# Sliding-window attention into a gated feed-forward: the third half's q and k transposed by TensorE instead of the DMA crossbar, and the fourth half's loads placed behind wo

## The chip, the cores and the metric

The kernel runs on one core of one Trainium2 chip. The metric is the device time of one execution in microseconds (us), and less is better. The kernel before takes 266.46 us (median of three runs, 266.06 to 266.63). The profile comes from one further execution, which has a time of its own.

## The reference, cut to what matters

Four batches, eight heads, 768 positions and a head size of 64. Every query sees eight global keys and the 96 most recent ones, with a linear bias by distance. The result is laid out as 3072 tokens of 512 numbers and goes through a feed-forward of width 1536 with a gate.

```
keep   = is_global | ((rel >= 0) & (rel < 96))        # rel = query position - key position
scores = q @ k.T / sqrt(64) - slope_of_head * dist
a      = softmax(where(keep, scores, -1e9))
x      = (a @ v) laid out as [3072, 512]
out    = (relu(x @ w_gate) * (x @ w_val)) @ w_out
```

All inputs and the output are float32; the kernel computes in bf16 with float32 accumulation.

## The kernel before, in words

**Halves and chunks.** The queries are cut into eight halves `s` = 0..7 of 384 positions, two for each batch. A half's attention gives `xT[s]`, 512 by 384, and this is the input of feed-forward chunk `c = s`. A chunk has 24 first-layer items (a `gate` and a `val` for each of twelve groups of 128 columns, four matmuls of 384 columns each, L479 and L489) and six `outp` items (six matmuls of 512 columns each, L498), of which two make one block of 128 output rows. The result of an `outp` pair is copied to `osb` (two buffers) and stored by SP. The first-layer weights come in three groups of four (`wg[0..2]`, `wv[0..2]`), the second-layer weight `wo_sb` in one DMA of its own, all issued by POOL, which also casts them to bf16 on the way.

**How q and k get into shape.** The matmul that makes the scores needs q and k with the head dimension on the partitions, and they arrive with positions there. There are two ways in the kernel.
- Halves 0 and 1: `piece_cast` casts a pair of heads to bf16, `piece_t` transposes it with six TensorE matmuls against the identity (L281) into an `av_ps` bank, and DVE copies q to `qT` (L285) and the keys to their places in `kT` (`put_keys`, L265 to L271).
- Halves 2 to 7: `piece_cast_k` and `piece_cast_q` cast on POOL into `kc` and `qz` (L289, L297; `qz` has zeros beside each head, so that two heads of a pair go through one matmul), three DMA transposes each on SP's queue bring them to `kN` and `qT` (`piece_xk` L300, `piece_xq` L304), and `piece_order` copies the keys from `kN` to `kT`, on DVE for half 2 and on POOL for the others.

**Attention itself.** Halves 0 and 1 add the bias with matmuls (`piece_bias`, L330) ahead of the score matmuls (`piece_score`, L347); later halves multiply by a mask after the exponential (`piece_qk`, L365 to L377). `piece_av` (L393) and `piece_av_wide` (L427) multiply by v; the sums go through ACT as Ln and Exp of its negative, and DVE multiplies the result into `xT` (L410, L438).

**What sets the order.** The schedule is written out by hand: the order of the calls is the order on each engine, and SP, POOL, DVE, ACT and PE each work through their own list. `weave` runs a list of feed-forward items and puts other pieces between them, each at a share of the list's estimated time. After half 0's attention there are these stages:
- **first weave**: group 0 of chunk 0 and the first two items of group 1 (ten items), with the attention of half 1;
- **second weave**: group 0 of chunk 1, the rest of group 1 of chunk 0, and group 1 of chunk 1 (22 items); in the kernel before it holds nothing else for PE;
- **third weave**: group 2 of both chunks (16 items), then the `outp` items of both (12 items), with the attention of half 2;
- **then** one weave for each of the chunks 2 to 7, with the attention of the next half and the casts and transposes of the one after.

Between the first and the second weave stand the preparations for halves 2 and 3, which mostly concern POOL and SP: weight group 2, q and k of halves 2 and 3 (`load_qk_after`: a tiny memset of the buffer on POOL, behind which the loads on SP wait), the zeros, the casts and transposes of both halves, v, and the load of `wo_sb`.

Of the kernel before, what the change touches and what calls it, by code (L numbers as in the profile page):

```python
# [15 lines left out]
def kernel(  # L16
# [12 lines left out]
    nc = tc.nc  # L29

    B, H, S, D = q.shape
# [8 lines left out]
    NN = 3  # L40
# [200 lines left out]
    def piece_cast(s, p):  # L241
        qk = cast_pool.tile([128, 2, NN, 2, D], BF16, name="qk")
        cast_of[s, p] = qk
        for i, src in ((1, ks_of[s]), (0, qs_of[s])):
            copy = nc.gpsimd.tensor_copy
            if s == 0:
                copy = (nc.vector.tensor_copy, nc.scalar.copy, nc.scalar.copy, nc.vector.tensor_copy)[p]
            elif p > 0:
                copy = (nc.vector.tensor_copy, nc.scalar.copy)[p % 2]
            copy(  # L250
                qk[:, i].rearrange("t n e d -> t e n d"),
                src[:, 2 * p : 2 * p + 2, :].rearrange("t e (n d) -> t e n d", n=NN))

    def put_keys(copy, copy_small, kt, src, half):

        tk = src.rearrange("d (n p) -> d p n", n=NN)

        def put(j0, j1, p0, r0, r1):
            o = kt[:, j0:j1, r0:r1].rearrange("d j (p n) -> d j p n", n=NN)
            np_ = (r1 - r0) // NN  # L260
            i_ = tk[:, p0 : p0 + (j1 - j0) * np_, :].rearrange("d (j p) n -> d j p n", j=j1 - j0)
            return o, i_

        if half == 0:
            copy(*put(0, 3, 0, NG, 128))  # L265
            copy_small(*put(3, 4, 120, NG, NG + 24))
            copy_small(kt[:, :, 0:NG], kt[:, 0:1, NG : 2 * NG].to_broadcast([128, NT, NG]))
        else:
            copy(*put(4, 6, 32, NG, 128))
            copy_small(*put(3, 4, 0, NG + 24, 128))  # L270
            copy_small(*put(6, 7, 112, NG, NG + 48))  # L271

    def piece_t(s, p):
        b, half = divmod(s, 2)
        kt = kT[b % 2][p]
        qk = cast_of[s, p]
        tp = av_psum.tile([128, 512], FP32, name="av_ps")
        tp = tp[:, 0:QH].bitcast(BF16).rearrange("d (i t) -> d i t", i=2)
        for i in range(2):
            for n in range(NN):  # L280
                nc.tensor.matmul(tp[:, i, n * 128 : (n + 1) * 128],  # L281
                                 lhsT=qk[:, i, n],
                                 rhs=ident, is_transpose=True,
                                 start=(i == 0 and n == 0), stop=(i == 1 and n == NN - 1))
        nc.vector.tensor_copy(qTb[s][:, p, 0, :], tp[:, 0, :])  # L285
        put_keys(nc.vector.tensor_copy, nc.vector.tensor_copy, kt, tp[:, 1, :], half)

    def piece_cast_k(s, p):
# [18 lines left out]

    def piece_order(s, p):
        b, half = divmod(s, 2)
        copy = nc.vector.tensor_copy if s == 2 else nc.gpsimd.tensor_copy  # L310
        put_keys(copy, copy, kT[b % 2][p], kNb[s % 2][:, p], half)

    def early_pieces(s):
        out = [(0.0, lambda p=p: piece_cast_k(s, p)) for p in range(HP)]
# [122 lines left out]
            xT_of[s] = xt_pool.tile([128, N_DC, QH], BF16, name="xT")  # L437
        nc.vector.tensor_tensor(xT_of[s][:, p, :], av[1][:, 0:QH], rc, op=ALU.mult)  # L438

    def attention_pieces(s):  # L440
        T = lambda p: [(0.34, lambda: piece_t(s, p))]
        QK = lambda p: [(0.18, lambda g=g: piece_qk(s, p, g)) for g in range(3)]
        AW = lambda p: [(0.58, lambda: piece_av_wide(s, p))]
        C = lambda p: [(0.0, lambda: piece_cast(s, p))]
        BI = lambda p, *gs: [(0.2, lambda g=g: piece_bias(s, p, g)) for g in gs]
        SC = lambda p, *gs: [(0.2, lambda g=g: piece_score(s, p, g)) for g in gs]
        X = lambda *fs: [(0.0, f) for f in fs]
        if s == 0:
            return (C(0) + X(lambda: load_v_globals(0), lambda: load_v(0, 0), lambda: load_v(0, 1),
                             lambda: load_v(0, 2), lambda: load_v(0, 3), lambda: load_w_group(0))  # L450
                    + C(1) + T(0) + BI(0, 0, 1) + C(2) + T(1) + SC(0, 0, 1) + BI(1, 0) + SC(1, 0) + C(3) + T(2)
                    + BI(1, 1) + SC(1, 1) + BI(2, 0) + T(3) + X(lambda: copy_v_globals(0, 1, 4))
                    + SC(2, 0) + BI(2, 1) + SC(2, 1)
                    + BI(3, 0) + SC(3, 0) + BI(3, 1) + SC(3, 1)
                    + AW(0) + AW(1) + X(lambda: load_qk_after(1, nc.vector, True)) + AW(2)
                    + AW(3) + X(second_pools, lambda: warm(4)))
        if s == 1:
            return (C(1) + C(2) + T(0) + BI(0, 0, 1) + T(1) + C(3) + SC(0, 0, 1) + T(2) + BI(1, 0) + SC(1, 0) + BI(1, 1)
                    + SC(1, 1) + T(3) + BI(2, 0) + SC(2, 0) + BI(2, 1) + AW(0) + SC(2, 1) + BI(3, 0)
                    + SC(3, 0) + AW(1) + BI(3, 1) + SC(3, 1) + AW(2) + AW(3))  # L460
        AV = lambda p: [(0.29, lambda e=e: piece_av(s, p, e)) for e in range(2)]
        g = QK(3)
        a = AV(2)
        return (QK(0) + QK(1) + AV(0) + QK(2) + AV(1) + g[0:1] + a[0:1] + g[1:2] + a[1:2] + g[2:3]
                + [(0.0, lambda: None)] * 2 + AV(3))
# [51 lines left out]
    def spread(items, first, last):  # L517

        n = len(items)
        return [(first + (i + 0.5) / n * (last - first), f) for i, (_, f) in enumerate(items)]  # L520
# [25 lines left out]
    f1_0, f2_0 = ffn_pieces(0)  # L546
    f1_1, f2_1 = ffn_pieces(1)
    G = [slice(2 * GW * i, 2 * GW * (i + 1)) for i in range(N_FC // GW)]
    g0 = f1_0[G[0]]
    weave(g0[0::2] + g0[1::2] + f1_0[G[1]][0:2], spread(attention_pieces(1), 0.4, 0.98))  # L550
    other_pools()
    load_w_group(2)
    load_qk_after(2, nc.gpsimd)
    load_qk_after(3, nc.gpsimd)
    for p in range(HP):
        nc.gpsimd.memset(kT[1][p][:, 3, 32:128].bitcast(mybir.dt.uint32), 0)
        nc.gpsimd.memset(kT[1][p][:, 6, NG + 48 : 128].bitcast(mybir.dt.uint32), 0)
    nc.gpsimd.memset(vbuf[1][:, NT - 1, :].bitcast(mybir.dt.uint32), 0)
    for i in range(2):
        nc.gpsimd.memset(qz[i].rearrange("t n p e z -> t (n p e z)").bitcast(mybir.dt.uint32), 0)  # L560
    for j in range(NT):
        fill_ones(nc.gpsimd, 1, j)
    load_v_globals(1)
    for _, f in early_pieces(2)[:-HP]:
        f()
    spread_v_globals(1)
    load_v_half(2)
    e3 = early_pieces(3)[:-HP]
    for _, f in e3[:HP]:
        f()  # L570
    load_w(wo_sb, moe_w_out, 0, DM)
    for _, f in e3[HP:]:
        f()
    load_v_half(3)
    weave(f1_1[G[0]] + f1_0[G[1]][2:] + f1_1[G[1]],
          [(0.1 + 0.1 * h, lambda h=h: mask(h)) for h in range(H)])
    weave(f1_0[G[2]] + f1_1[G[2]] + f2_0 + f2_1,
          [(0.02 + 0.05 * p, lambda p=p: piece_order(2, p)) for p in range(HP)],
          spread(attention_pieces(2), 0.25, 0.9), [(0.95, lambda p=p: piece_order(3, p)) for p in range(HP)],
          [(0.55 + 0.05 * j, lambda j=j: fill_ones(nc.vector, 0, j)) for j in range(NT)])  # L580

    for c in range(2, NHALF):
# [44 lines left out]
```

## Time and profile before

| what | value |
|---|---|
| time, median of three runs | 266.46 us (266.06 to 266.63) |
| the profiled execution: its own time | 264.71 us |
| its span, first to last instruction | 262.7 us |
| PE busy (TensorE matmuls) | 243.4 us, 93% of the span |
| ACT busy | 159.6 us, 61% |
| DVE busy | 127.5 us, 49% |
| POOL busy | 85.7 us, 33% |
| mean granted TensorE clock | 0.985 of full |
| moved by DMA | 34.31 MB, 131 GB/s over the span |

The profiled execution lasted 2.0 us longer than its span, and 1.75 us less than the median of the timed runs. A row of the timeline gives the start, the time from the first start to the last end of a group of like instructions, the engine, the line, the operation with its tiles, the count, and in brackets the idle time just before and what ended it. Matmuls overlap in the pipe, so the cost of one group of matmuls is read from its start to the start of the next. A row of the windows gives, for a stretch of time, the busy time of PE, PE's weight loads, DVE, ACT and POOL with the number of instructions, then the granted clock, the mean busy share of the DMA engines (it can exceed 1 where packets overlap) and the GB/s.

### The profile page before, as it was taken

How to read it: one execution, taken by the hardware profiler on the slowest of the kernel's cores; microseconds unless marked ns; L12 is line 12 of the kernel's file. 1: busy time of each engine (PE TensorE's matmuls, PEld its weight loads, DVE VectorE, ACT ScalarE, POOL GpSimd, SP SyncE). 2: the span in 40 equal slices, each digit the busy share in tenths (PEclk: the TensorE clock that was granted, in tenths of full speed). 3: DMA queues.
4: the chain of work that ended last, by engine and by line, in shares of the span. 5: the costliest groups of instructions: out<-in, count | busy, mean ns of one | idle time of the engine just before them, and what ended most of it. 6: DMA issues, size and time to landing. Idle time of an engine off the chain costs nothing.

```text
span 262.7 us, 4849 instructions
## 1 busy us (share of the span) xinstructions
PE 243.4 (93%) x1727; PEld 142.7 (54%) x1727; DVE 127.5 (49%) x328; ACT 159.6 (61%) x321; POOL 85.7 (33%) x213
## 2 busy tenths in 40 slices
PE   7888769995699999999999999999999999999993
PEld 3655555662345556655655566655665566556641
DVE  3646424472406556752667166625573356714410
ACT  5876575732438568755776477756875678653311
POOL 7808903990021516430164505800550000000000
PEclk9999999998979999999999999999999999999999
DMA  6999999999992496773744995864771200021012
GB/s 192 140 220 213 180 232 311 184 140 156 152 169 95 94 230 183 154 59 114 229 109 88 120 295 90 132 75 120 223 159 44 80 0 2 1 80 42 0 40 80
DMA packets 82264, 34.31 MB, mean 131 GB/s; under 512 B 58177, under 2 KB 79169, under 8 KB 82241
## 3 DMA queue, kind: packets, MB, share of 16 engines
q1 hardware_dynamic: 50384, 26.11, 40.8%
q0 software_dynamic: 31856, 7.91, 32.4%
q8 instruction: 13, 0.21, 0.4%
q14 instruction: 11, 0.08, 0.1%
HBM read 28.38 MB, written 6.29 MB: 132 GB/s over the span
## 4 chain that ended last, share of the span: by engine, by line
PE 66%; DMA 17%; ACT 6%; DVE 5%; POOL 2%; issue 2%; SPq 1%; ACTq 0%; DVEq 0%
PE ff_ps L498 24%; PE ff_ps L489 16%; PE ff_ps L479 15%; DMA qs<-in_q_dram 8%; DMA wo_sb<-in_moe_w_out_dram 7%; PE av_ps L393 5%; PE qk_ps L365 4%; DVE xT L410 2%; DMA ks<-in_k_dram 2%; SPq L131 1%; ACT es L352 1%; ACT rcp L407 1%; ACT lnd L402 1%; DVE ht L491 1%; POOL vbuf L155 1%
## 5 line engine op out<-in xcount | busy, mean ns | idle before, releaser
L489 PE MATMUL ff_ps<-xT,wv 128*128 128x384 bf16 x384 | 78.7, 328 | 2.1 <-DMA wv<-in_moe_w_val_dram 1.2
L479 PE MATMUL ff_ps<-xT,wg 128*128 128x384 bf16 x384 | 78.5, 327 | 1.5 <-DMA wg<-in_moe_w_gate_dram 1.2
L498 PE MATMUL ff_ps<-wo_sb,ht 128*128 128x512 bf16 x288 | 68.4, 384 | 2.9 <-DMA wo_sb<-in_moe_w_out_dram 2.9
L482 ACT ACTIVATE grelu<-ff_ps 128x384 bf16<-128x384 f32 x96 | 47.1, 490 | 35.2 <-PE ff_ps L479 18.0
L491 DVE TENSOR_TENSOR ht<-ff_ps,grelu 128x384 bf16<-128x384 f32 x96 | 53.2, 555 | 29.9 <-PE ff_ps L489 24.1
L479 PEld LDWEIGHTS <-wg 128*128 128x128 bf16 x384 | 36.5, 98 | 25.7 <-DMA wg<-in_moe_w_gate_dram 1.9
L489 PEld LDWEIGHTS <-wv 128*128 128x128 bf16 x384 | 36.3, 98 | 25.2 <-issue 3.1
L410 DVE TENSOR_TENSOR xT<-av_ps,rcp 64x384 bf16<-64x384 f32 x48 | 26.6, 555 | 46.4 <-ACT rcp L407 45.7
L368 ACT ACTIVATE es<-qk_ps 128x432 bf16<-128x432 f32 (+2 forms) x72 | 37.9, 528 | 18.3 <-PE qk_ps L365 16.4
L377 DVE TENSOR_TENSOR es<-es,m_all 128x432 bf16<-128x432 bf16 (+5 forms) x108 | 31.1, 316 | 30.8 <-ACT es L368 30.3
L498 PEld LDWEIGHTS <-ht 128*128 128x128 bf16 x288 | 27.1, 98 | 31.8 <-DMA wo_sb<-in_moe_w_out_dram 3.3
L503 ACT COPY osb<-ff_ps 128x512 f32<-128x512 f32 x24 | 14.1, 586 | 26.2 <-PE ff_ps L498 25.3
L402 ACT ACTIVATE lnd<-av_ps 64x384 f32<-64x384 f32 x48 | 23.3, 485 | 10.4 <-PE av_ps L393 9.6
L289 POOL CAST kc<-ks 128x384 bf16<-128x384 f32 x24 | 11.4, 521 | 54.7 <-DMA ks<-in_k_dram 47.6
L365 PE MATMUL qk_ps<-qT,kT 128*128 128x432 bf16 (+5 forms) x108 | 25.4, 292 | 2.6 <-DMA qT<-qz 2.6
L155 POOL DMA_DIRECT2D vbuf<-in_v_dram x28 | 24.4, 880 | 0.4 <-issue 0.3
L393 PEld LDWEIGHTS <-vbuf 128*128 128x128 bf16 x216 | 18.3, 99 | 8.1 <-issue 0.8
L393 PE MATMUL av_ps<-es,vbuf 128*128 128x216 bf16 (+4 forms) x216 | 21.5, 227 | 0.2 <-DVE xT L410 0.2
L365 PEld LDWEIGHTS <-kT 128*128 128x128 bf16 x108 | 10.7, 99 | 11.1 <-DMA qT<-qz 3.0
L297 POOL CAST qz<-qs 128x192 bf16<-128x192 f32 x48 | 14.6, 356 | 5.2 <-DMA qs<-in_q_dram 4.7
L407 ACT ACTIVATE rcp<-lnd 128x384 f32<-128x384 f32 x24 | 12.5, 523 | 0.8
L352 ACT ACTIVATE es<-qk_ps 128x864 bf16<-128x864 f32 (+3 forms) x16 | 10.6, 708 | 3.5 <-PE qk_ps L347 3.5
(77 smaller groups left out, 131.7 us busy)
## 6 DMA issues: line engine op xcount, KB each, us to landing
out_dram<-osb SPq DMA_DIRECT2D x24, 256.0 KB
ks<-in_k_dram SPq DMA_DIRECT2D x6, 768.0 KB
qs<-in_q_dram SPq DMA_DIRECT2D x6, 768.0 KB
vbuf<-in_v_dram POOLq DMA_DIRECT2D x24, 120.0 KB, 4.6
ks<-in_k_dram SPq DMA_DIRECT2D x8, 192.0 KB
qs<-in_q_dram SPq DMA_DIRECT2D x8, 192.0 KB
wg<-in_moe_w_gate_dram POOLq DMA_DIRECT2D x3, 512.0 KB, 7.8
wv<-in_moe_w_val_dram POOLq DMA_DIRECT2D x3, 512.0 KB, 10.8
```

The lines of the kernel that those rows point to most:

```text
L155: nc.gpsimd.dma_start(out=v_dst(b, NG + r0, NG + r0 + n, j), in_=v[b, :, KT * j + r0 : KT * j + r0 + n, :].rearrange("h p d -> p h d"))
L365: nc.tensor.matmul(ps[:, c : c + n_], lhsT=kt[:, j, :], rhs=qd[:, :, :, a : a + w], start=True, stop=True)
L368: nc.scalar.activation(es[:, 0:cols], ps[:, 0:cols], AF.Exp, bias=0.0, scale=scale)
L377: nc.vector.tensor_mul(e4, e4, mk)
L393: nc.tensor.matmul(av3[:, :, a : a + w], lhsT=vb[:, j, z0 : z0 + 128], rhs=es[:, c : c + NN * w].rearrange("k (n p) -> k n p", n=NN), star ...
L402: nc.scalar.activation(ln[o0 : o0 + 64], av[d0 : d0 + 64, 0:QH], AF.Ln, bias=0.0, scale=1.0)
L410: nc.vector.tensor_tensor(xT_of[s][r, p, :], av_of[s, p, e_][r, 0:QH], rc[r], op=ALU.mult)
L479: nc.tensor.matmul(psg[:, 0:QH], lhsT=w_of(wg, dc, fc), rhs=xT[:, dc, :], start=(dc == 0), stop=(dc == N_DC - 1))
L482: nc.scalar.activation(gr, psg[:, 0:QH], AF.Relu, bias=0.0, scale=1.0)
L489: nc.tensor.matmul(psv[:, 0:QH], lhsT=w_of(wv, dc, fc), rhs=xT[:, dc, :], start=(dc == 0), stop=(dc == N_DC - 1))
L491: nc.vector.tensor_tensor(ht[:, fc, :], psv[:, 0:QH], st[fc], op=ALU.mult)
L498: nc.tensor.matmul(ps2, lhsT=ht[:, fc, n * 128 : (n + 1) * 128], rhs=wo_sb[:, fc, :], start=(fc == 0), stop=(fc == N_FC - 1))
```

## The change

- `piece_cast` runs on POOL for all four pairs of half 2, and `piece_t` also serves half 2: it writes q in two copies of 64 partitions, one for each head of the pair, into a `qT[0]` whose other halves POOL has set to zero. The four `piece_t` of half 2 stand in the second weave at 0.50, 0.64, 0.78 and 0.92 of it. Half 2 no longer uses `kc`, `qz`, `kN`, the six DMA transposes and `piece_order`.
- q and k of half 2 are loaded in four pairs of heads (eight DMAs) instead of two whole DMAs.
- q and k of half 3 are no longer loaded at the start of the second weave, but at 0.25 of the third, behind a memset on DVE. Its casts, v, transposes and `piece_order` follow in the third weave, at 0.40 to 0.45, 0.45, 0.52 to 0.56 and 0.64 to 0.68, and 0.93 to 0.97.
- On POOL the load of `wo_sb` stands behind the casts and the v of half 2, and nothing of half 3 is ahead of it.
- In the first weave the four `val` items of group 0 and the two items of group 1 take other places among the attention pieces of half 1.
- The attention of half 2 starts at 0.20 of the third weave instead of 0.25.

```diff
@@ piece_cast
             if s == 0:
                 copy = (nc.vector.tensor_copy, nc.scalar.copy, nc.scalar.copy, nc.vector.tensor_copy)[p]
-            elif p > 0:
+            elif s == 1 and p > 0:
                 copy = (nc.vector.tensor_copy, nc.scalar.copy)[p % 2]
@@ piece_t
-        nc.vector.tensor_copy(qTb[s][:, p, 0, :], tp[:, 0, :])
+        if s < 2:
+            nc.vector.tensor_copy(qTb[s][:, p, 0, :], tp[:, 0, :])
+        else:
+            for e in range(2):
+                r = slice(64 * e, 64 * e + 64)
+                nc.vector.tensor_copy(qTb[s % 2][r, p, e, :], tp[r, 0, :])
@@ piece_order
-        copy = nc.vector.tensor_copy if s == 2 else nc.gpsimd.tensor_copy
-        put_keys(copy, copy, kT[b % 2][p], kNb[s % 2][:, p], half)
+        put_keys(nc.gpsimd.tensor_copy, nc.gpsimd.tensor_copy, kT[b % 2][p], kNb[s % 2][:, p], half)
@@ attention_pieces
-    def attention_pieces(s):
+    def attention_pieces(s, vals=(), more=()):
...
         if s == 1:
-            return (C(1) + C(2) + T(0) + BI(0, 0, 1) + T(1) + C(3) + SC(0, 0, 1) + T(2) + BI(1, 0) + SC(1, 0) + BI(1, 1)
-                    + SC(1, 1) + T(3) + BI(2, 0) + SC(2, 0) + BI(2, 1) + AW(0) + SC(2, 1) + BI(3, 0)
-                    + SC(3, 0) + AW(1) + BI(3, 1) + SC(3, 1) + AW(2) + AW(3))
+            v = [[x] for x in vals]
+            m = [[x] for x in more]
+            return (C(1) + C(2) + T(0) + BI(0, 0, 1) + v[0] + C(3) + T(1) + SC(0, 0, 1) + v[1] + T(2)
+                    + BI(1, 0) + SC(1, 0) + BI(1, 1) + SC(1, 1) + v[2] + T(3) + BI(2, 0) + SC(2, 0)
+                    + BI(2, 1) + AW(0) + v[3] + SC(2, 1) + BI(3, 0) + SC(3, 0) + AW(1)
+                    + BI(3, 1) + SC(3, 1) + m[0] + AW(2) + m[1] + AW(3))
@@ the stages
-    g0 = f1_0[G[0]]
-    weave(g0[0::2] + g0[1::2] + f1_0[G[1]][0:2], spread(attention_pieces(1), 0.4, 0.98))
+    for _, f in f1_0[0:2 * GW:2]:
+        f()
+    for _, f in attention_pieces(1, f1_0[1 : 2 * GW : 2], f1_0[2 * GW : 2 * GW + 2]):
+        f()
     other_pools()
     load_w_group(2)
-    load_qk_after(2, nc.gpsimd)
-    load_qk_after(3, nc.gpsimd)
+    load_qk_after(2, nc.gpsimd, True)
...
-    for i in range(2):
-        nc.gpsimd.memset(qz[i].rearrange("t n p e z -> t (n p e z)").bitcast(mybir.dt.uint32), 0)
+    for e in range(2):
+        nc.gpsimd.memset(qTb[0][64 - 64 * e : 128 - 64 * e, :, e, :].bitcast(mybir.dt.uint32), 0)
...
     load_v_globals(1)
-    for _, f in early_pieces(2)[:-HP]:
-        f()
+    for p in range(HP):
+        piece_cast(2, p)
+    load_v_half(2)
+    load_w(wo_sb, moe_w_out, 0, DM)
     spread_v_globals(1)
-    load_v_half(2)
-    e3 = early_pieces(3)[:-HP]
-    for _, f in e3[:HP]:
-        f()
-    load_w(wo_sb, moe_w_out, 0, DM)
-    for _, f in e3[HP:]:
-        f()
-    load_v_half(3)
+    for i in range(2):
+        nc.gpsimd.memset(qz[1 - i].rearrange("t n p e z -> t (n p e z)").bitcast(mybir.dt.uint32), 0)
+    e3 = early_pieces(3)
+    ck, xk, cq, xq, od = e3[0:HP], e3[HP : HP + NN], e3[HP + NN : 2 * HP + NN], e3[2 * HP + NN : -HP], e3[-HP:]
     weave(f1_1[G[0]] + f1_0[G[1]][2:] + f1_1[G[1]],
-          [(0.1 + 0.1 * h, lambda h=h: mask(h)) for h in range(H)])
+          [(0.1 + 0.1 * h, lambda h=h: mask(h)) for h in range(H)],
+          [(0.5 + 0.14 * p, lambda p=p: piece_t(2, p)) for p in range(HP)])
     weave(f1_0[G[2]] + f1_1[G[2]] + f2_0 + f2_1,
-          [(0.02 + 0.05 * p, lambda p=p: piece_order(2, p)) for p in range(HP)],
-          spread(attention_pieces(2), 0.25, 0.9), [(0.95, lambda p=p: piece_order(3, p)) for p in range(HP)],
+          spread(attention_pieces(2), 0.2, 0.9), [(0.25, lambda: load_qk_after(3, nc.vector))],
+          spread(ck + cq, 0.4, 0.45), [(0.45, lambda: load_v_half(3))],
+          spread(xk, 0.52, 0.56), spread(xq, 0.64, 0.68), spread(od, 0.93, 0.97),
           [(0.55 + 0.05 * j, lambda j=j: fill_ones(nc.vector, 0, j)) for j in range(NT)])
```

What this does to the lists of the engines is seen at three places. The first is POOL's list behind the global rows of v (L141) up to the end of v for half 3; `kc` and `qz` are the operands of the DMA transposes, `qk` that of `piece_t`, and a row with a count stands for that many calls. In the kernel before:

```order
L289 CAST kc_112<-ks 128x2x3x64 x4
L297 CAST qz_110<-qs 128x3x64 x8
L155 DMA vbuf_96<-in_v_dram 120x8x64 x4
L289 CAST kc_113<-ks 128x2x3x64 x4
L172 DMA wo_sb<-in_moe_w_out_dram 128x12x512
L297 CAST qz_111<-qs 128x3x64 x8
L155 DMA vbuf_96<-in_v_dram 120x8x64 x2
```

In the changed kernel (the last of the four pairs of casts is shown, the three like it stand ahead):

```order
L250 CAST qk<-ks 128x2x3x64
L250 CAST qk<-qs 128x2x3x64
L155 DMA vbuf_96<-in_v_dram 120x8x64 x4
L172 DMA wo_sb<-in_moe_w_out_dram 128x12x512
L578 MEMSET qz_111 128x1536
L294 CAST kc_113<-ks 128x2x3x64 x4
L302 CAST qz_111<-qs 128x3x64 x8
L155 DMA vbuf_96<-in_v_dram 120x8x64 x2
```

The casts of half 3's k no longer stand ahead of the load of `wo_sb`; all of half 3's work is behind it.

The second place is SP's list, from the last loads of half 2 to the first stores of the output. In the kernel before, where `kc_112`, `qz_110` belong to half 2 and `kc_113`, `qz_111` to half 3:

```order
L131 DMA ks<-in_k_dram 128x8x192
L131 DMA qs<-in_q_dram 128x8x192
L300 DMA_TRANSPOSE kN_108<-kc_112 128x4x128 x3
L304 DMA_TRANSPOSE qT_106<-qz_110 128x8x128 x3
L146 DMA vbuf_96<-vbuf_96 8x8x64 x6
L300 DMA_TRANSPOSE kN_109<-kc_113 128x4x128 x3
L304 DMA_TRANSPOSE qT_107<-qz_111 128x8x128 x3
L504 DMA out_dram<-osb 128x512 x6
```

In the changed kernel:

```order
L146 DMA vbuf_96<-vbuf_96 8x8x64 x6
L131 DMA ks<-in_k_dram 128x8x192
L131 DMA qs<-in_q_dram 128x8x192
L511 DMA out_dram<-osb 128x512
L305 DMA_TRANSPOSE kN_109<-kc_113 128x4x128 x2
L511 DMA out_dram<-osb 128x512
L305 DMA_TRANSPOSE kN_109<-kc_113 128x4x128
L309 DMA_TRANSPOSE qT_107<-qz_111 128x8x128
L511 DMA out_dram<-osb 128x512
L309 DMA_TRANSPOSE qT_107<-qz_111 128x8x128 x2
L511 DMA out_dram<-osb 128x512 x3
```

The six transposes of half 2 are gone, and those of half 3, which stood ahead of all stores of the first two chunks, now stand between them, behind the loads of their own half.

The third place is DVE's list from the last `piece_t` of half 1 to the keys of the first pair of half 2; `ht` is the product of a `val` item, `xT` that of an attention pair. In the kernel before:

```order
L271 COPY kT_3_101<-av_ps 128x48
L438 TENSOR_TENSOR xT<-av_ps,rcp 128x384 x2
L491 TENSOR_TENSOR ht<-ff_ps,grelu 128x384
L438 TENSOR_TENSOR xT<-av_ps,rcp 128x384 x2
L491 TENSOR_TENSOR ht<-ff_ps,grelu 128x384 x11
L265 COPY kT_0_102<-kN_108 128x3x120
```

In the changed kernel:

```order
L271 COPY kT_3_101<-av_ps 128x48
L442 TENSOR_TENSOR xT<-av_ps,rcp 128x384
L498 TENSOR_TENSOR ht<-ff_ps,grelu 128x384
L442 TENSOR_TENSOR xT<-av_ps,rcp 128x384 x2
L498 TENSOR_TENSOR ht<-ff_ps,grelu 128x384
L442 TENSOR_TENSOR xT<-av_ps,rcp 128x384
L498 TENSOR_TENSOR ht<-ff_ps,grelu 128x384 x5
L290 COPY qT_106<-av_ps 64x384 x2
L265 COPY kT_0_102<-av_ps 128x3x120
```

There is one more `val` product among the attention pairs of half 1 than before, and the one that stood between the second and the third pair (the `val` of group 1) stands between the third and the fourth. The keys of half 2 come from the PSUM bank of `piece_t` instead of `kN`, after five of the eleven products of the second weave instead of after all of them.

## The prediction

> **What bounds the kernel now.** I read the page first, then PE's waits, then stretches of time, then PE's timeline where the waits lie. The page:
>
> ```profile
> span 262.7 us, 4849 instructions
> PE 243.4 (93%) x1727; PEld 142.7 (54%) x1727; DVE 127.5 (49%) x328; ACT 159.6 (61%) x321; POOL 85.7 (33%) x213
> ```
>
> PE is the bound, and 19.3 us of the span are left that it is not busy. PE's longest waits for DMA:
>
> ```profile
> PE ff_ps L498 <- DMA wo_sb<-in_moe_w_out_dram: 2.9, 1, 2.9
> PE qk_ps L365 <- DMA qT<-qz: 2.6, 1, 2.6
> ```
>
> Each happens once, for `wo_sb` and for the transposed q of half 2, both in the third weave. Windows of the first weave and around the two waits (PE, PEld, DVE, ACT and POOL busy, then granted clock, DMA share, GB/s):
>
> ```profile
> 16.13:39.84 23.71, 18.59 (x234) 12.28 (x231) 10.57 (x30) 14.94 (x28) 12.76 (x32) 1.00 1.19 216
> ...
> 61.45:69.70 8.25, 5.62 (x27) 2.83 (x26) 2.21 (x7) 3.27 (x7) 0.00 (x0) 0.79 1.33 168
> 69.70:77.67 7.97, 5.05 (x23) 2.45 (x23) 1.77 (x5) 1.57 (x5) 1.97 (x7) 0.79 1.60 149
> 77.67:93.66 15.99, 15.77 (x95) 8.13 (x94) 8.37 (x23) 10.92 (x22) 5.43 (x10) 1.00 0.55 117
> ```
>
> The first weave leaves PE 5.1 us idle, at a full clock. In the two rows in the middle two things cost time: the waits, and a granted clock of 0.79 over each stretch. In the last row, still the third weave, the clock is 1.00 and PE is busy for 15.77 of 15.99 us. PE's timeline there:
>
> ```profile
> 60.64 0.81 PE L479 MATMUL ff_ps<-xT,wg 128*128 128x384 bf16 x4
> 64.09 0.54 PE L365 MATMUL qk_ps<-qT,kT 128*128 128x432 bf16 x1 [2.63 <-DMA qT<-qz]
> ...
> 67.32 0.81 PE L489 MATMUL ff_ps<-xT,wv 128*128 128x384 bf16 x4
> ...
> 68.62 0.35 PE L365 MATMUL qk_ps<-qT,kT 128*128 128x432 bf16 x1
> 68.80 0.81 PE L489 MATMUL ff_ps<-xT,wv 128*128 128x384 bf16 x4
> 69.45 0.35 PE L365 MATMUL qk_ps<-qT,kT 128*128 128x432 bf16 x1
> 72.72 1.71 PE L498 MATMUL ff_ps<-wo_sb,ht 128*128 128x512 bf16 x6 [2.92 <-DMA wo_sb<-in_moe_w_out_dram]
> ...
> 77.67 1.46 PE L498 MATMUL ff_ps<-wo_sb,ht 128*128 128x512 bf16 x6
> ...
> 79.33 1.46 PE L498 MATMUL ff_ps<-wo_sb,ht 128*128 128x512 bf16 x6
> 80.63 0.31 PE L365 MATMUL qk_ps<-qT,kT 128*128 128x288 bf16 x2
> 80.78 0.42 PE L393 MATMUL av_ps<-es,vbuf 128*128 128x216 bf16 x4
> 81.05 1.46 PE L498 MATMUL ff_ps<-wo_sb,ht 128*128 128x512 bf16 x6
> ```
>
> From start to start at full clock: a gate or val item 0.65 (68.80 to 69.45), a score matmul 0.18 (68.62 to 68.80) or 0.15 for the pair of small ones (80.63 to 80.78), an `outp` item 1.30 (79.33 to 80.63), an AV piece 0.27 (80.78 to 81.05).
>
> **The two waits of the third weave, with their slow clock.** The item at 60.64 costs 0.65, so PE could go on at 61.29; it does at 64.09: 2.80 lost. Between 64.09 and 67.32 stand three scores and two items, 0.18 + 0.65 + 0.18 + 0.65 + 0.15 = 1.81; they take 3.23: 1.42 lost to the clock. At 69.45 + 0.18 = 69.63 PE could start on `outp`; it does at 72.72: 3.09. From there to 77.67 stand two `outp` items, a score pair and two AV pieces, 2.60 + 0.15 + 0.54 = 3.29; they take 4.95: 1.66. In all 2.80 + 1.42 + 3.09 + 1.66 = 8.97 us. The change aims at both waits. The first goes if q of half 2 is there in time, the second if `wo_sb` is; each takes its slow clock along, since the clock is 1.00 in the windows without such a wait.
>
> **The first weave.** Its end on PE and DVE before:
>
> ```profile
> 35.58 0.82 PE L489 MATMUL ff_ps<-xT,wv 128*128 128x384 bf16 x4 [1.22 <-DMA wv<-in_moe_w_val_dram]
> ...
> 38.02 0.49 PE L427 MATMUL av_ps<-es,ones 128*64 128x216 bf16 x10 [0.39 <-ACT lnd L433]
> ...
> 40.49 0.81 PE L489 MATMUL ff_ps<-xT,wv 128*128 128x384 bf16 x4
> ```
>
> ```profile
> 39.72 0.56 DVE L438 TENSOR_TENSOR xT<-av_ps,rcp 128x384 bf16<-128x384 f32 x1 [0.60 <-PE av_ps L427]
> ```
>
> The val of group 1 waits for its weight until 35.58, and two more attention pairs follow, one after the other, up to the last `xT` at 39.72 + 0.56 = 40.28. From 38.02, where that last pair's sums begin, it is 2.26 us. In the changed kernel this val stands between the third and the fourth pair, and a waiting PE has the deferred val of group 0 to do earlier. If the weight still lands at 35.58, the last sums begin at 36.23 and `xT` ends at 38.49: 1.8 us sooner. The ends of this cost are 0.65 worse (one more item ahead of half 1's last scores, and ACT then sets the end) and 3.0 better (the weight lands by 34.36, when PE first asked for it, 1.22 sooner). I take 1.8, since the rows chain from a landing that nothing in the change delays. The second weave begins in effect at 40.49 - 0.65 = 39.84 before and at 38.04 after.
>
> **The second weave: added work.** Six transposes of 128x128, as half 1 has them:
>
> ```profile
> 25.54 0.50 PE L281 MATMUL av_ps<-ident,qk 128*128 128x128 bf16 x6
> 25.88 0.51 PE L330 MATMUL qk_ps<-dd,sid 128*128 128x216 bf16 x4
> ```
>
> Start to start 0.34, four times: 1.36 us on PE, which is the bound here (upper end: the 0.50 that the group lasts, four times, 2.00). A page of the Trainium skill speaks against this edit: "TensorE: Matmul & The Clock Gate", Part 4: PE-mode transpose, gives some 275 ns for one transpose within a kernel and says that transposes don't count as activity for the clock; by that price the 24 would take 6.6 us, and the time would come out 5.2 us above my sum. The trace disagrees: six start within 0.34 us, in a window with a clock of 1.00.
>
> DVE takes the results out of PSUM beside the val products:
>
> ```profile
> 5.29 0.36 DVE L285 COPY qT<-av_ps 128x384 bf16<-128x384 bf16 x1 [0.91 <-PE av_ps L281]
> 5.57 0.52 DVE L265 COPY kT<-av_ps 128x360 bf16<-128x360 bf16 x1
> ```
>
> From 5.29 these run to about 6.3, 1.0 us; with q in two copies (0.28 more) 1.3. A val product needs its DVE turn before its bank is due, two items (1.3 us) after the val ends; the item between the transposes and that end gives 0.65 more. So 1.3 + 0.56 of DVE fits into 1.95, narrowly, and I cost it at nothing; without that cover up to 0.4 per pair, 1.6 in all.
>
> The casts must be done first. POOL before:
>
> ```profile
> 40.26 1.85 POOL L289 CAST kc<-ks 128x384 bf16<-128x384 f32 x4 [6.95 <-DMA ks<-in_k_dram]
> 45.46 2.39 POOL L297 CAST qz<-qs 128x192 bf16<-128x192 f32 x8 [3.35 <-DMA qs<-in_q_dram]
> 47.79 3.64 POOL L155 DMA_DIRECT2D vbuf<-in_v_dram  x4
> ...
> 53.21 1.04 POOL L172 DMA_DIRECT2D wo_sb<-in_moe_w_out_dram  x1
> ```
>
> All of k and q of half 2 is there at 45.46, and k alone, half of the bytes, at 40.26; by pairs k and q alternate. Two pairs are thus ready at about 41.2, the last at 45.46 plus two casts of 1.85 / 4 = 46.4. The four `piece_t` stand after 11, 15, 18 and 21 items: 38.04 + 7.15 = 45.2, then 48.1, 50.4 and 52.7. No wait, with 4 and more to spare. The third weave begins at 38.04 + 22 x 0.65 + 1.36 = 53.70.
>
> **`wo_sb`.** POOL comes to it at 46.4 + 3.64 = 50.0 instead of 53.21. How long it takes to land is the main unknown:
>
> ```profile
> wv<-in_moe_w_val_dram POOLq DMA_DIRECT2D x3, 512.0 KB, 10.8
> wo_sb<-in_moe_w_out_dram POOLq DMA_DIRECT2D x1, 1536.0 KB, 19.5
> ```
>
> ```profile
> DMA to landing us min/median/max: 9.3/10.8/17.8
> ```
>
> ```profile
> 26.21 0.78 POOL L172 DMA_DIRECT2D wv<-in_moe_w_val_dram  x1
> ```
>
> The middle fence is of tile `wv`, the last row of POOL's timeline: `wv`'s middle load landed at 35.58, the last at 26.21 + 17.8 = 44.0. Between them lie two weights of 512 KB, so 8.4 us for 1 MB with q and k loading beside it; 1.5 MB make 12.6. The upper end is the 19.5 of before, when DMA transposes of halves 2 and 3 fell into that time; a shorter one would change nothing. I take 12.6, as the only neighbours left are q and k of half 3, late: 50.0 + 1.0 + 12.6 = 63.6. It is due after 16 items and six score pieces, 53.70 + 10.4 + 1.0 = 65.1. A page of the Trainium skill speaks against this step too: "Advanced Engine Details and Errata", X-Bar Transpose (TRN2), says that transposing DMAs are as fast as ordinary ones, so taking them away would clear little; by it the first rival below is the forecast. The windows disagree: 149 GB/s at a DMA share of 1.60 with the transposes, 117 at 0.55 without most of them.
>
> **Half 3.** Its loads start at 0.25 of the third weave, near 60.5; q is due at the first score of the next weave. The next half's chain before, on SP and POOL:
>
> ```profile
> 94.86 0.43 SPq L131 DMA_DIRECT2D ks<-in_k_dram  x1
> ...
> 106.96 3.94 SPq L304 DMA_TRANSPOSE qT<-qz  x3
> ```
>
> From the loads to the last transpose issued that is 16.0 us, so here 76.5; its place at 0.64 and more of the weave, behind five `outp` items and some 2.9 us of attention, gives 53.70 + 10.4 + 6.5 + 2.9 + 3.94 = 77.4. Due: the third weave lasted from 39.84 + 14.3 = 54.14 to 93.66, 39.52; without 8.97 it ends at 53.70 + 30.55 = 84.2. The landing behind the issue has 6.8 us, and I cost it at nothing. SP waits for the casts with stores behind it, but the two `osb` buffers cover two blocks, 5.2 us.
>
> **The sum**, against the profiled execution: 8.97 + 1.8 - 1.36 = 9.4 less, 264.71 to 255.3; against the median, which lies 1.75 higher, 266.46 - 9.4 = 257.1. The later weaves wait for nothing that the change touches.
>
> **The rivals.**
> - *`wo_sb` as slow as before* (the rule on transposes would have it so). It lands at 50.0 + 19.5 = 69.5, PE waits 4.4 and pays 1.66 of clock: 257.1 + 6.1 = 263.2. For it: `wv` and `wo_sb`, both from POOL's queue, were late before. Against: no transposes are in flight between 50.0 and 65. 0.10.
> - *Nothing from the first weave*: ACT's chain sets the end, 258.9. For it: PE waited there for ACT's `lnd`. 0.15.
> - *The clock falls with each `piece_t`* (the rule on transposes and the clock): 1.42 each, 5.7 in all, 262.8. Against: half 1 at full clock. 0.03.
> - *Slower: q of half 3 comes late.* Half 2's chain before, on SP:
>
> ```profile
> 27.09 0.37 SPq L131 DMA_DIRECT2D ks<-in_k_dram  x1
> ...
> 49.27 6.39 SPq L304 DMA_TRANSPOSE qT<-qz  x3
> ```
>
> From the loads to the first score at 64.09 it took 37.0 us (8.4 of them behind the last issue at 55.66). From 60.5 that gives 97.5; PE waits 13.3 at the first score of half 3 and pays 1.42 of clock: 257.1 + 14.7 = 271.8. It ends slower if q lands after 84.2 + 9.4 - 1.4 = 92.2. Against: that chain had half 3's loads and the weights in its way. 0.05.
>
> **How the numbers follow.** The forecast has 0.66, and 0.01 is for a mix that ends at no change. It lies between 255.9 (3.0 in the first weave) and 259.3 (transposes at 2.00 and DVE without cover, 0.6 + 1.6). The second rival reaches from 258.9 to 259.6 (0.65 worse than before), and with those two costs half paid, 1.1, to 260.7: the top of the range; forecast and second rival hold 0.81. A measurement tells 0.2% (0.5 us) from no change. The forecast and the first three rivals end faster: 0.94; same 0.01, slower 0.05.
>
> **What would show it.** Right: no wait of PE on `qT` or `wo_sb` before 85, a clock of 1.00 from 53 to 84, 24 transposes at about 0.34 a group, the third weave some 30.5 long, the first weave's last `xT` near 38.5. Wrong: an `outp` waiting for `wo_sb`, a first score of half 3 waiting for `qT`, SP waiting for casts with `osb` copies held up, or gate items spaced by more than 0.65 around `piece_t`.

## The result and the profile after

Beside the kernel before, the changed kernel took 255.69 us against 266.26 (medians of four runs each): a ratio of 0.9628, 95% interval 0.9571 to 0.9686, or 8.4 to 11.4 us saved. On another chip it was 257.95 (six runs) against 264.63 (eleven), 0.9758 (0.9727 to 0.9789). A ratio is taken over undisturbed executions only, so it needn't be the quotient of the medians. The two intervals don't overlap. The kernel before ranges over 5.8 us on that other chip (262.55 to 268.31), for reasons that no run traced; the changed one ranges over 1.6 on the first chip and 1.5 on the other, and two reasons are found below. The profiled executions give 264.71 and 255.49 us, 9.2 less, and the spans 262.7 and 253.4.

The forecast was 257.1, in a range of 255.9 to 260.7, from 266.46 before. The first ratio turns 266.46 into 256.5 and the second into 260.0; the bare median of 255.69 lies just under the range.

The page of the changed kernel, and the one wait of PE for a DMA that is left (PE's waits):

```profile
span 253.4 us, 4902 instructions
...
PE 241.4 (95%) x1751; PEld 142.9 (56%) x1751; DVE 131.3 (52%) x338; ACT 159.4 (63%) x321; POOL 87.9 (35%) x209
```

```profile
PE ff_ps L496 <- DMA wv<-in_moe_w_val_dram: 0.7, 1, 0.7
```

Its second weave, its third weave and the weave of chunk 2 as windows:

```profile
38.09:53.97 15.88, 15.39 (x110) 9.65 (x110) 10.68 (x28) 9.01 (x19) 10.30 (x13) 1.00 0.97 129
53.97:84.22 30.25, 30.25 (x185) 16.70 (x184) 16.92 (x46) 18.13 (x37) 12.96 (x31) 1.00 0.98 191
84.22:112.90 28.68, 28.45 (x193) 16.92 (x192) 16.27 (x41) 19.65 (x39) 11.76 (x29) 1.00 0.89 154
```

The third weave, 39.5 us before, is 30.25, with PE busy throughout at a clock of 1.00. PE's timeline at the places of the prediction's steps:

```profile
35.60 0.82 PE L496 MATMUL ff_ps<-xT,wv 128*128 128x384 bf16 x4 [0.65 <-DMA wv<-in_moe_w_val_dram]
...
38.58 0.32 PE L486 MATMUL ff_ps<-xT,wg 128*128 128x384 bf16 x1 [0.83 <-DVE xT L442]
38.74 0.81 PE L496 MATMUL ff_ps<-xT,wv 128*128 128x384 bf16 x4
...
45.24 0.50 PE L281 MATMUL av_ps<-ident,qk 128*128 128x128 bf16 x6
45.57 0.81 PE L496 MATMUL ff_ps<-xT,wv 128*128 128x384 bf16 x4
...
52.83 0.50 PE L281 MATMUL av_ps<-ident,qk 128*128 128x128 bf16 x6
...
65.47 1.46 PE L505 MATMUL ff_ps<-wo_sb,ht 128*128 128x512 bf16 x6
...
84.22 0.81 PE L486 MATMUL ff_ps<-xT,wg 128*128 128x384 bf16 x4
84.87 0.37 PE L369 MATMUL qk_ps<-qT,kT 128*128 128x144 bf16 x2
```

No bracket stands at the first `outp` item (65.47) nor at half 3's first score (84.87). `wo_sb` was issued by POOL at 50.10 and landed 12.5 us later; SP loaded half 3 from 62.30 and issued its last transpose until 80.70:

```profile
50.10 1.04 POOL L172 DMA_DIRECT2D wo_sb<-in_moe_w_out_dram  x1
```

```profile
62.30 0.38 SPq L131 DMA_DIRECT2D ks<-in_k_dram  x1
...
76.82 3.88 SPq L309 DMA_TRANSPOSE qT<-qz  x2
```

### The profile page after: what moved, and what is told of

It reads as the page before. It is cut to its first block, busy times and chain, and to the rows that moved or that the text cites. A ratio compares the mean times of both kernels' runs of the same rounds, so it can differ in the third digit from the quotient of the medians.

```text
span 253.4 us, 4902 instructions
## 1 busy us (share of the span) xinstructions
PE 241.4 (95%) x1751; PEld 142.9 (56%) x1751; DVE 131.3 (52%) x338; ACT 159.4 (63%) x321; POOL 87.9 (35%) x209
## 4 chain that ended last, share of the span: by engine, by line
PE 78%; DMA 7%; ACT 6%; DVE 5%; SPq 2%; issue 1%; ACTq 0%; POOL 0%; POOLq 0%
PE ff_ps L505 25%; PE ff_ps L496 21%; PE ff_ps L486 21%; PE av_ps L397 5%; PE qk_ps L369 4%; DMA wv<-in_moe_w_val_dram 4%; DMA qs<-in_q_dram 3%; DVE xT L414 2%; SPq L131 2%; DVE ht L498 1%; ACT rcp L411 1%; PE av_ps L281 1%; ACT grelu L489 1%; ACT lnd L406 1%; ACT es L356 1%
## 5 line engine op out<-in xcount | busy, mean ns | idle before, releaser
L489 ACT ACTIVATE grelu<-ff_ps 128x384 bf16<-128x384 f32 x96 | 47.0, 490 | 33.6 <-PE ff_ps L486 19.5
L505 PE MATMUL ff_ps<-wo_sb,ht 128*128 128x512 bf16 x288 | 67.1, 379 | 0.0
L498 DVE TENSOR_TENSOR ht<-ff_ps,grelu 128x384 bf16<-128x384 f32 x96 | 53.9, 565 | 23.1 <-PE ff_ps L496 18.0
L381 DVE TENSOR_TENSOR es<-es,m_all 128x432 bf16<-128x432 bf16 (+5 forms) x108 | 32.5, 328 | 22.4 <-ACT es L372 22.0
L294 POOL CAST kc<-ks 128x384 bf16<-128x384 f32 x20 | 9.8, 535 | 57.4 <-DMA ks<-in_k_dram 57.4
L369 PE MATMUL qk_ps<-qT,kT 128*128 128x432 bf16 (+5 forms) x108 | 24.8, 286 | 0.0
L302 POOL CAST qz<-qs 128x192 bf16<-128x192 f32 x40 | 12.7, 369 | 3.5 <-DMA qs<-in_q_dram 3.2
L411 ACT ACTIVATE rcp<-lnd 128x384 f32<-128x384 f32 x24 | 12.5, 522 | 0.8
```

The costliest lines, as they stand in the source:

```text
L369: nc.tensor.matmul(ps[:, c : c + n_], lhsT=kt[:, j, :], rhs=qd[:, :, :, a : a + w], start=True, stop=True)
L381: nc.vector.tensor_mul(e4, e4, mk)
L489: nc.scalar.activation(gr, psg[:, 0:QH], AF.Relu, bias=0.0, scale=1.0)
L498: nc.vector.tensor_tensor(ht[:, fc, :], psv[:, 0:QH], st[fc], op=ALU.mult)
L505: nc.tensor.matmul(ps2, lhsT=ht[:, fc, n * 128 : (n + 1) * 128], rhs=wo_sb[:, fc, :], start=(fc == 0), stop=(fc == N_FC - 1))
```

## The experiments

The theory: half 2's DMA transposes made its first score late and, with those of half 3, slowed `wo_sb`; each wait brought a slow clock; the first weave gave 1.8. The main rivals: TensorE's transposes aren't needed once half 3 is deferred; deferring isn't needed once half 2 is off the crossbar.

**The first weave alone undone.**

```diff
-    for _, f in f1_0[0:2 * GW:2]:
-        f()
-    for _, f in attention_pieces(1, f1_0[1 : 2 * GW : 2], f1_0[2 * GW : 2 * GW + 2]):
-        f()
+    g0 = f1_0[G[0]]
+    weave(g0[0::2] + g0[1::2] + f1_0[G[1]][0:2], spread(attention_pieces(1), 0.4, 0.98))
```

> The changed kernel with the first weave in its old order. My sum gives the order of the first weave 1.8 us: this run should take 1.8 us more than the changed kernel's 255.7, so 257.5, with the last xT of half 1 near 40.3 instead of 38.5 and nothing else moved. The rival says that the first weave's gain is given back later (the later stages have slack of their own): 255.7.

Measured: 257.58 against 264.10 (ratio 0.9804, 0.9748 to 0.9860); profiled span 255.6, 2.2 more than the changed kernel's. The last `xT` ends at 40.31 + 0.56 = 40.9, with `wv` waited for until 36.18. PE's wait and DVE's last `xT`:

```profile
36.18 0.82 PE L493 MATMUL ff_ps<-xT,wv 128*128 128x384 bf16 x4 [1.21 <-DMA wv<-in_moe_w_val_dram]
```

```profile
40.31 0.56 DVE L442 TENSOR_TENSOR xT<-av_ps,rcp 128x384 bf16<-128x384 f32 x1 [0.60 <-PE av_ps L431]
```

By the traces, the theory; the size 2.2 instead of 1.8, of which 0.6 is the later `wv`. The changed kernel itself did not run on this chip, nor beside the next three runs, so the size compares two chips. Against the next two runs, which share this chip and have the new first weave, the old one costs 0.9 us, and the intervals of the ratios overlap.

**Half 3 early again, half 2 still on TensorE.**

```diff
     load_qk_after(2, nc.gpsimd, True)
+    load_qk_after(3, nc.gpsimd)
...
     load_v_half(2)
+    for _, f in ck:
+        f()
     load_w(wo_sb, moe_w_out, 0, DM)
+    for _, f in xk + cq + xq:
+        f()
+    load_v_half(3)
```

> The changed kernel, half 2 still transposed by TensorE, but half 3 loaded, cast and transposed as early as in the kernel before, its k casts ahead of wo on POOL. My theory: wo is issued at about 53 and shares its time with six DMA transposes, so that it lands at 53.3 + 16 = 69 or so, 3.5 to 4 us late, and PE's clock falls behind it: 255.7 + 4 + 1.7 = 261.4, with no wait for qT. The rival, that the transposes cost wo nothing and only its place on POOL counts: it lands in 12.5 us, at 65.8, and the time is 255.7 to 256.5.

Measured: 256.64 against 264.10 (0.9766, 0.9693 to 0.9838), span 252.9. My theory's 261.4 fell: PE waits neither for `wo_sb` nor for `qT`. POOL, PE and tile `wo_sb` of this run:

```profile
47.95 1.84 POOL L294 CAST kc<-ks 128x384 bf16<-128x384 f32 x4
49.75 1.04 POOL L172 DMA_DIRECT2D wo_sb<-in_moe_w_out_dram  x1
```

```profile
64.83 1.46 PE L505 MATMUL ff_ps<-wo_sb,ht 128*128 128x512 bf16 x6
```

```profile
DMA to landing us min/median/max: 14.7/14.7/14.7
```

The q and k of both halves had landed sooner than I took from the kernel before, so that `wo_sb` was issued at 49.75, and with six transposes beside it took 14.7 us and not 16: it is there at 64.4, 0.4 before its turn. So the rival that deferring half 3 isn't needed, once half 2 is off the crossbar, stands.

**Only half 3's loads early** (the one line `load_qk_after(3, nc.gpsimd)` moved back, casts and transposes late).

> The changed kernel, with only the loads of half 3's q and k as early as before; its casts and transposes stay where the change puts them. My theory says that wo is held up by POOL's list and by the transposes, not by these loads, which are done by about 51: wo is issued at 50 and lands by 64, the time stays at 255.7. The rival, that the deferred loads are what counts: wv of group 1 and 2 and the pairs of half 2 land later, the first weave loses about 1 us and wo is late again, 258 or more.

Measured: 256.71 against 264.10 (0.9788, 0.9733 to 0.9843), span 254.3, `wo_sb` in 12.8 us, no wait for it. As the theory says.

**Half 2 on the crossbar again, half 3 deferred.**

```diff
-    for p in range(HP):
-        piece_cast(2, p)
+    for _, f in early_pieces(2)[:-HP]:
+        f()
     load_v_half(2)
     load_w(wo_sb, moe_w_out, 0, DM)
...
-          [(0.5 + 0.14 * p, lambda p=p: piece_t(2, p)) for p in range(HP)])
+          )
```

> The changed kernel with half 2 through the DMA crossbar as before (whole loads, casts into kc and qz, six transposes), half 3 behind wo as in the change. My theory: the first score of half 2 waits for qT again, if less than the 2.8 us of before since half 3's loads are out of its way, and wo shares its time with half 2's transposes: 1.5 to 3 us of waits and 1.4 to 3 of slow clock, less 1.4 for the TensorE transposes that are gone: about 258. The rival, that deferring half 3 alone is enough and the TensorE transposes are pure cost: 255.7 - 1.4 = 254.3.

The whole loads of half 2, the early zeros of `qz` and `piece_order` on DVE come back with it. Measured: 258.93 against 264.10 (0.9863, 0.9796 to 0.9931), span 258.4; the six executions lie between 256.83 and 260.19, and the profiled one, 260.17, is at the upper end. Here is the wait that the rival denied, and the clock behind it (PE's timeline, then windows):

```profile
63.18 0.52 PE L370 MATMUL qk_ps<-qT,kT 128*128 128x432 bf16 x1 [4.18 <-DMA qT<-qz]
```

```profile
57.00:62.00 5.00, 2.00 (x13) 0.98 (x10) 1.83 (x6) 0.98 (x2) 0.00 (x0) 1.00 1.72 122
62.00:66.00 4.00, 2.82 (x9) 1.31 (x10) 1.01 (x3) 1.06 (x2) 0.00 (x0) 0.57 1.32 208
```

`wo_sb`, issued at 52.36, took 17.3 us and landed at 69.7, just ahead of its turn, which the first wait had put off to 70.1. So `qT` was late without any load of half 3 in its way (they start at 66.44). It landed 9.0 us behind the end of its last issue, with `wo_sb` in flight beside it; no run tells which of the two held the other.

**The changed kernel again, and each TensorE transpose done twice** (on one chip; the loop holds the same six transposes, into `ex`).

```diff
+        if s == 2:
+            ex = av_psum.tile([128, 512], FP32, name="av_ps")
+            for i in range(2):
...
         tp = av_psum.tile([128, 512], FP32, name="av_ps")
```

> The changed kernel once more, as the measure for the three runs beside it: 255.5 to 257, no wait of PE for qT or wo_sb.

> The changed kernel with each of the four groups of six TensorE transposes of half 2 done twice, the extra ones into a bank that nothing reads. My sum has 0.34 us for a group at full clock: 1.36 us more than the changed kernel beside it, clock 1.00 throughout. The rival, the rule that a transpose costs some 275 ns and doesn't keep the clock up: 6.6 us more, or the clock below 1.00 around them.

Measured: 257.95 (0.9758, 0.9727 to 0.9789), above the 255.5 to 257 that was expected, and, doubled, 257.24 (0.9754, 0.9705 to 0.9804): no difference that these runs can tell. The trace of the doubled one has the price:

```profile
44.62 0.50 PE L282 MATMUL av_ps<-ident,qk 128*128 128x128 bf16 x6
44.96 0.50 PE L290 MATMUL av_ps<-ident,qk 128*128 128x128 bf16 x6
45.29 0.81 PE L505 MATMUL ff_ps<-xT,wv 128*128 128x384 bf16 x4
```

Each extra group takes 0.34 us, 1.36 in all, and the clock is 1.00 from 38 to 84: 6.6 us are ruled out. By the traces, what hides the 1.36 in the times is the swing of the plain run beside it: its first transposes stand at 46.88, against 44.62 here, and it has two places that are 1.6 and 1.0 us worse than in the first profile (PE, DVE and POOL):

```profile
37.24 0.82 PE L496 MATMUL ff_ps<-xT,wv 128*128 128x384 bf16 x4 [1.58 <-DMA wv<-in_moe_w_val_dram]
...
51.42 0.81 PE L496 MATMUL ff_ps<-xT,wv 128*128 128x384 bf16 x4 [1.02 <-DVE ht L498]
```

```profile
48.15 0.54 DVE L265 COPY kT<-av_ps 128x360 bf16<-128x360 bf16 x1
...
48.72 2.62 DVE L267 COPY kT<-kT 128x56 bf16<-128x56 bf16 x1
```

```profile
46.68 3.63 POOL L155 DMA_DIRECT2D vbuf<-in_v_dram  x4
50.30 1.04 POOL L172 DMA_DIRECT2D wo_sb<-in_moe_w_out_dram  x1
```

`wv` lands 1.6 us later here. And DVE's small copy within `kT`, 0.18 us elsewhere, lasts until POOL has issued `wo_sb`, 48.72 + 2.62 = 50.30 + 1.04, while the copy out of PSUM ahead of it has its usual length under the same POOL work. The `ht` product behind it comes late, and PE waits. The copy isn't held each time: in another trace below it took 0.25 us while POOL issued the loads of v.

**The two items of group 1 behind the last attention pairs, and a val item ahead of the first transposes besides** (same chip).

```diff
-                    + BI(3, 1) + SC(3, 1) + m[0] + AW(2) + m[1] + AW(3))
+                    + BI(3, 1) + SC(3, 1) + AW(2) + AW(3) + m[0] + m[1])
```

> The changed kernel with the two items of group 1 moved from before the last two attention pairs of half 1 to behind them, so that the last pair no longer waits for wv of group 1 and the items cover the way from its sums to xT. Theory: the first weave's end is set by the landing of wv and by the 0.8 us in which PE then waits for xT; the second weave begins about 1.2 us sooner: 1.2 us less than the changed kernel beside it. The rival, that ACT's chain of es, Ln and Exp sets the end: no change.

> As the run before, and the first val item of group 0 stands ahead of half 1's first transposes again, each further val one place earlier. Theory: it fills 0.65 of the 1.24 us in which PE waits for the casts there, and half 1's last scores come one item sooner: 1.2 + 0.6 = 1.8 us less than the changed kernel beside it. The rival, that PE then waits at the place where the last val stood: only 1.2 less.

Measured: 255.42 (0.9679, 0.9642 to 0.9717) and 255.80 (0.9682, 0.9651 to 0.9714); the changed kernel beside them 257.95, and its interval (0.9727 to 0.9789) doesn't overlap. So the kernel with the first edit is some 2.5 us faster on that chip. In its trace PE waits for no `wv` any more, and the second weave's first transposes stand at 45.26, against 46.88 for the changed kernel there and 45.24 in the first profile, where `wv` landed early:

```profile
45.26 0.50 PE L281 MATMUL av_ps<-ident,qk 128*128 128x128 bf16 x6
```

The edit takes away the exposure to `wv`, 1.6 us in these two traces; another 1.0 is the wait for `ht` that this trace happens not to have. With an early `wv` it gains nothing by the traces, as the rival says: PE then waits twice 0.65 us for `xT`. The second edit adds nothing (its transposes begin at 45.08).

**The small copy on ACT instead of DVE**, on top of the first of these edits, and that kernel again beside it (the added argument is the engine of the last copy alone).

```diff
-        put_keys(nc.vector.tensor_copy, nc.vector.tensor_copy, kt, tp[:, 1, :], half)
+        put_keys(nc.vector.tensor_copy, nc.vector.tensor_copy, kt, tp[:, 1, :], half,
+                 nc.scalar.copy if s == 2 else None)
```

> The kernel with the two items of group 1 behind the last attention pairs, once more, as the measure for the run beside it: 255 to 256.5; DVE's small copy of the global keys (kT from kT, 0.18 us when alone) lasts up to some 2.5 us while POOL issues v and wo_sb or clears qz.

> As the run beside it, but the small copy of the global keys of half 2 within kT (SBUF to SBUF) is done by ACT instead of DVE. Theory: of what DVE does for the TensorE transposes only this copy is held up by POOL, since it alone reads and writes SBUF; the copies out of PSUM run through. Then DVE's copies and products in the second weave keep their usual times, PE never waits for ht there (0.4 to 1.5 us in the runs so far), and the time is 0.3 to 1 us less and varies less. The rival: POOL holds up DVE's copies out of PSUM as well, or ACT's gates come late in its place: no change or slower.

Measured: 256.62 (0.9778, 0.9712 to 0.9845) and 257.48 (0.9798, 0.9733 to 0.9862): no gain. The changed kernel did not run on this chip, so the gain of the edit before is not confirmed here; in its trace half 1's first transposes wait 2.57 us for their casts, against 1.35 before, and the second weave's stand at 46.58 without any wait for `wv`. In the same trace the copy is held by POOL's clearing of `qz`, 51.51 + 2.71 against 51.46 + 2.72 (DVE, POOL):

```profile
51.51 2.71 DVE L267 COPY kT<-kT 128x56 bf16<-128x56 bf16 x1
```

```profile
51.46 2.72 POOL L578 MEMSET qz<- 128x1536 uint32 x2
```

On ACT it isn't held, beside the same clearing (ACT, POOL):

```profile
51.23 0.24 ACT L267 COPY kT<-kT 128x56 bf16<-128x56 bf16 x1 [1.16 <-DVE kT L265]
```

```profile
50.47 2.71 POOL L579 MEMSET qz<- 128x1536 uint32 x2
```

But ACT now stands in its own list until DVE has written the keys, and the next gate comes late (ACT, then PE):

```profile
54.12 0.24 ACT L267 COPY kT<-kT 128x56 bf16<-128x56 bf16 x1 [1.80 <-DVE kT L265]
```

```profile
55.24 0.81 PE L497 MATMUL ff_ps<-xT,wv 128*128 128x384 bf16 x4 [0.85 <-ACT grelu L490]
```

That POOL's work holds DVE's copy is shown; the cure traded one wait for another.

**PE's waits of the kernel before filled with matmuls.**

```diff
+    def fill(n):
+        t = av_psum.tile([128, 512], FP32, name="av_ps")
+        for _ in range(n):
+            nc.tensor.matmul(t, lhsT=wg[0][:, 0, 0:128], rhs=wg[0][:, 0, :], start=True, stop=True)
...
+    f20 = [(0.0, lambda: fill(13))] + f2_0
...
+          [(0.2645, lambda: fill(12))], spread(attention_pieces(2), 0.25, 0.9),
```

> The kernel before, with PE kept busy in its two waits of the third weave: 12 matmuls of 512 columns that nothing reads ahead of half 2's first score, 13 ahead of the first outp item. My theory: the slow clock behind each wait comes from PE's idling, so it stays at 1.00 and 1.42 + 1.66 = 3.1 us are saved, the waits themselves stay (the filling takes their place): the kernel before less 3.1. The rival, that the clock falls for another cause at that time: no change, or slower where the filling outlasts the wait.

Measured: 264.13 against 265.26, ratio 1.0012 (0.9949 to 1.0075): no difference shown, though the clock stays up (windows, then PE's timeline):

```profile
61.45:69.70 8.25, 7.77 (x43) 3.95 (x42) 3.19 (x9) 3.68 (x8) 0.00 (x0) 1.00 1.47 160
69.70:77.67 7.97, 5.54 (x34) 2.81 (x33) 0.44 (x3) 1.71 (x4) 1.10 (x5) 1.00 1.77 135
```

```profile
64.33 0.36 PE L370 MATMUL qk_ps<-qT,kT 128*128 128x432 bf16 x1 [0.48 <-DMA qT<-qz]
...
73.65 1.47 PE L503 MATMUL ff_ps<-wo_sb,ht 128*128 128x512 bf16 x6 [2.43 <-DMA wo_sb<-in_moe_w_out_dram]
```

The DMA share is as high as in the prediction's windows (1.47 and 1.77 against 1.33 and 1.60), and the clock is 1.00 all the same: the slow clock comes with PE's idling, and the rival is out. The filling didn't cover the second wait: PE idled for its last 2.43 us, and the clock stayed at 1.00 behind it, where an idle stretch of 2.63 had brought it down in the kernel before. The 3.1 us were wrongly added up: what PE gains behind the first wait it only waits longer for `wo_sb`, whose landing is a point in time (here 21.0 us after its issue). By this reckoning at most the 1.66 of the second could be saved, and the times don't show even that.

**Half 3 later by 0.20 of the third weave** (loads at 0.45, casts 0.60 to 0.65, transposes 0.72 to 0.76 and 0.84 to 0.88).

> The changed kernel with all of half 3 0.20 of the third weave later (loads at 0.45 instead of 0.25, and casts, v and transposes with them), some 6.8 us. By the prediction's own reckoning the transposed q of half 3 has 6.8 us of slack: 0 to 1.4 us more than the changed kernel. By the trace of the changed kernel, where the loads start at 62.1 and the last transpose is issued at 80.7, the slack is 1 to 2 us: PE waits 5 to 6 us for qT at the first score of half 3 and pays some 1.4 us of slow clock, 6 to 8 us more than the changed kernel, 262 to 264.

Measured: 265.18 against 265.26, ratio 1.0050 (0.9994 to 1.0105), span 261.2: the whole gain is gone. The forecast from the trace, 262 to 264, is met by the profiled execution (262.93) and missed by the median. PE, SP, and the window behind:

```profile
91.11 0.38 PE L369 MATMUL qk_ps<-qT,kT 128*128 128x144 bf16 x2 [4.55 <-DMA qT<-qz]
```

```profile
86.04 2.96 SPq L309 DMA_TRANSPOSE qT<-qz  x2
```

```profile
92.00:100.00 8.00, 8.00 (x45) 4.54 (x44) 5.39 (x14) 4.64 (x10) 7.36 (x15) 0.81 1.60 250
```

`qT` is there 2.1 us after the last issue ends (89.00 to 91.11). If the landing takes as long in the changed kernel, that makes 80.70 + 2.1 = 82.8, with 84.87 as its due time: a slack of 2.1.

## Why the prediction was right, point by point

By the traces, the third weave got 9.27 us shorter, the end of the first came 1.75 sooner, and the second got 1.58 longer: 9.4 in all, as forecast, and 9.3 by the spans. That it fits so closely is in part luck: misses of 0.3 in the third weave and 0.2 in the second cancel, and in these two executions `wv` landed at the same time, 35.58 and 35.60. On the other chip the ratio makes 6.4 us.

- **The waits and their clock, 8.97.** Right in size: the third weave is 30.25 us long and ends at 84.22; 84.2 was forecast. `wo_sb` didn't take the 19.5 us of the first rival. The addition hid an order: the two waits aren't independent. Had only `qT` come in time, PE would by this have waited longer for `wo_sb`. The sum held because both went.
- **The first weave, 1.8.** The last `xT` ends at 38.53 (38.49 forecast), and the second weave begins in effect at 38.74 - 0.65 = 38.09; 38.04 was forecast. It holds where `wv` lands at 35.6 and fails by 1.6 where it lands at 37.2. "A landing that nothing in the change delays" was right, and the landing itself swings; that it came at 35.60, as before, was luck.
- **TensorE's transposes, 1.36.** Right: 0.33 to 0.34 for each group, at 45.24 to 52.83 (45.2 to 52.7 forecast), also when doubled, and the clock kept up. The rival with the falling clock is out.
- **DVE's copies at nothing.** The step that failed, though it moves the sum little: PE loses 0.25 us in the first profile (two items spaced 0.75 and 0.80 in place of 0.65) and waits 0.8 to 1.3 in one place in four others. I had reckoned DVE's own time and not what else can hold it: POOL.
- **`wo_sb`, 12.6 from 50.0.** Right but for 1.0 us: with an issue of 1.0 and then 12.6 it was to land at 63.6, and it landed at 62.6, 12.5 behind the start of its issue. The landing times order themselves by what transposes run beside it: 12.4 to 13.2 without, 14.7 with half 3's six, 17.3 with half 2's six, 19.5 and 21.0 with both. In the experiments their other traffic differs too, so this is an order, not a price for each. The two windows that I had compared by their GB/s had different loads to move, and show no rate.
- **Half 3, slack 6.8.** Mis-sized: its loads began at 62.3 and not at 60.5, since the memset on DVE stands behind a mask product that waits for ACT, and its last transpose was issued at 80.70 and not 77.4. That left 4.2 us for the landing and not 6.8, of which the landing needs 2.1 if it goes as in the last run. It needed 8.4 behind the last issue for half 2 in the kernel before, and 9.0 in the run with half 2 on the crossbar, so the margin hangs on what else is in flight. The slower rival's mechanism is real: 7.9 us more cost the whole gain.
- **What the change's parts are worth.** On one chip, against the same 264.10, the change takes 256.64 without half 3's deferral, 257.58 without the new first weave and 258.93 without TensorE's transposes. So the last part is the one that is missed most, by some 2.3 us, though the intervals of the ratios still overlap. It doesn't carry the whole: what is left without it still saves 1.4%. The parts overlap, and no run gives a price to each. That deferring half 3 gains anything once half 2 is off the crossbar isn't shown; `wo_sb` is then there 2.9 us before its turn (62.6, 65.47) instead of 0.4, and half 3 has less to spare.

## What to carry to other kernels

Two waits on one engine are not two savings when the second is for a landing fixed in time: ask what PE would reach next. Moving a transpose from DMA to an engine that is the bound can pay, if its real price in the stream (0.34 us for six here) is below the wait that it removes. A copy that costs 0.2 us can cost 2.7 where it shares something with an engine that is "off the path": look at what runs beside it, not only at its length.

## What the runs showed of the hardware that was not expected

- DVE's copy from SBUF to SBUF (56 columns, bf16) took 0.18 us alone and up to 2.78 while POOL issued DMAs or cleared a tile, ending with POOL's work; copies from PSUM kept their 0.53 us under it, and the products with one PSUM operand their 0.55 to 0.56 in the run with the copy on ACT. It wasn't held each time (0.25 under the same DMA issues), and took 0.35 beside POOL's casts in the kernel before. This fits the Trainium skill, "SBUF — State Buffer", Who interferes with whom: DVE's two-port modes, which such copies can enter, and POOL share one pair of ports, and whichever issues first has it for its whole instruction. Here the copy was held over more than one POOL instruction, which that rule alone doesn't give.
- PE's clock fell after an idle stretch of only 2.63 us; it stayed at 1.00 where the wait was filled, and behind an idle stretch of 2.43.
- A 1.5 MB load that landed 12.4 to 13.2 us after its issue with no DMA transposes beside it took 19.5 and 21.0 where those of two halves were issued around it; other traffic differed too.
